# Streamed weights repacked in DRAM, so that rows which the 16 DMA engines are thought to move together lie side by side

## Chip, cores, metric

One core of a Trainium2 chip. The metric is the time of one execution on the device, in microseconds (us). All runs whose times are compared here are in the fast state (the probe e5, a single run, is read from its profile alone), and all outputs agreed with the reference.

## The reference, cut to what matters

Two branches over the same 2048 tokens of width 640, mixed by a gate. Branch A is sliding-window attention. Branch B is the one that matters: 64 segments of 32 tokens, each with 8 memory rows that come from the segment before, so the segments run one after the other, each through all of the weights.

```python
for s in range(n_seg):                                # 64 serial steps
    h = concatenate([mem, xs], axis=1)                # 40 rows x 640
    q = einsum('btd,dhe->bhte', h, Wq)                # 640 x (32*192); Wk, Wv alike
    ...
    o = einsum('bhte,hed->btd', o, Wo)                # (32*192) x 640
    mem = o[:, :M, :]                                 # goes into the next step
return g * a + (1 - g) * b
```

## The kernel before

Wq, Wk, Wv and Wo, in bfloat16, are not all kept in SBUF. Most tiles of 128 rows stay resident; 21 (11 of q, k and v, 10 of o) are packed once into a DRAM tensor, and every step loads them again, from the sync engine's queue into a ring of four slots.

```python
WQ, WO = 4 * 384, 2 * D                # 1536 columns (3072 B a row), 1280 (2560 B a row)

class Weights:
    def __init__(self, nc, dram, Wq, Wk, Wv, Wo, streamed):
        ...
        self.packed = dram.tile([len(streamed), P, WQ], BF, name="w_packed")

    def copy(self, u, dst, engine):
        kind, g, c = u
        if kind != "o":
            engine.dma_start(dst, self.src[kind][c, :, g * WQ:(g + 1) * WQ])
            return
        for r in range(2):
            i, b = divmod(2 * c + r, 3)
            for a in range(2):
                engine.dma_start(dst[64 * a:64 * a + 64, r * D:(r + 1) * D], self.Wo[8 * g + 2 * i + a, 64 * b:64 * b + 64, :])

    def dram_of(self, u):
        return self.packed[self.slot[u], :, 0:self.width(u)]
    ...

# in branch_B
    sb = {
        "w": (4, [P, WQ]), ...                     # the ring: 4 slots
    }
    def load_w(u):
        if u not in weights.slot:
            return None
        b = sc.buf("w")
        sc.op("SP", 100 + 0.78 * weights.width(u), lambda: nc.sync.dma_start(tile_of(b)[:, 0:weights.width(u)], weights.dram_of(u)),
              writes=[b])
        return b

STREAMED = {"q": ((4,), (4,), (4,), (4,)), "k": ((4,), (4,), (4,), (4,)), "v": ((), (4,), (4,), (4,)),
            "o": ((2, 5), (1, 3, 5), (1, 3, 5), (2, 5))}
```

Of the kernel before, what the change touches and what calls it, by code (L numbers as in the profile page):

```python
# [9 lines left out]
BF = mybir.dt.bfloat16  # L10
# [252 lines left out]
P = 128  # L263
KT = 5
D = 640


class Sched:
# [9 lines left out]
    def __init__(self, bufs):  # L278
        self.bufs, self.made, self.ops = bufs, {t: [] for t in bufs}, []
# [85 lines left out]
WQ, WO = 4 * 384, 2 * D  # L365
# [3 lines left out]
class Weights:  # L369
# [5 lines left out]
    def __init__(self, nc, dram, Wq, Wk, Wv, Wo, streamed):  # L375
        self.nc = nc
        self.src = {k: W.rearrange("(kt p) h e -> kt p (h e)", p=P) for k, W in (("q", Wq), ("k", Wk), ("v", Wv))}
        self.Wo = Wo
        self.slot = {u: n for n, u in enumerate(streamed)}
        self.packed = dram.tile([len(streamed), P, WQ], BF, name="w_packed")  # L380
        self.resident = [(k, g, c) for k in KINDS for g in range(4) for c in range(PARTS[k]) if (k, g, c) not in self.slot]
        self.tiles = {}

    def copy(self, u, dst, engine):
        kind, g, c = u
        if kind != "o":
            engine.dma_start(dst, self.src[kind][c, :, g * WQ:(g + 1) * WQ])
            return
        for r in range(2):
            i, b = divmod(2 * c + r, 3)  # L390
            for a in range(2):
                engine.dma_start(dst[64 * a:64 * a + 64, r * D:(r + 1) * D], self.Wo[8 * g + 2 * i + a, 64 * b:64 * b + 64, :])

    def load_resident(self, pool, u, engine):
        t = pool.tile([P, self.width(u)], BF, name="w_%s%d%d" % u)
# [5 lines left out]
        return WO if u[0] == "o" else WQ  # L401

    def dram_of(self, u):
        return self.packed[self.slot[u], :, 0:self.width(u)]

    def pack(self, u, engine):
        self.copy(u, self.dram_of(u), engine)

    def get(self, ring, u):
        if u in self.tiles:  # L410
# [59 lines left out]
def branch_B(ctx, tc, xa_dram, xbqk, xbv, mem0, weights, xo_dram):  # L470
    nc = tc.nc
# [49 lines left out]
    sc = Sched({t: n for t, (n, _) in sb.items()} | {t: n for t, (n, _) in kept.items()} | ps)  # L521

    def tile_of(b, shape=None, dtype=BF, name=None):
        t = b["tag"]
        if b["tile"] is None:
            if t in kept:
                b["tile"] = still[t][b["n"] % kept[t][0]]
            elif t in sb:
                b["tile"] = pools[t].tile(sb[t][1], BF, name=f"t_{t}", tag=t)
            else:  # L530
                b["tile"] = pools[t].tile(shape, dtype, name=name or f"p_{t}", tag=t)
        return b["tile"]
# [28 lines left out]
    def load_w(u):  # L561
        if u not in weights.slot:
            return None
        b = sc.buf("w")
        sc.op("SP", 100 + 0.78 * weights.width(u), lambda: nc.sync.dma_start(tile_of(b)[:, 0:weights.width(u)], weights.dram_of(u)),
              writes=[b])
        return b

# [18 lines left out]
    def chunk(kind, s, g):  # L587
        hT = hts[s][0]
        b = sc.buf("mm")
        wb = [load_w((kind, g, kt)) for kt in range(KT)]  # L590
        kts = [kt for kt in range(KT) if wb[kt] is None] + [kt for kt in range(KT) if wb[kt]]

        def f(kt):
            t = tile_of(b, [P, 512], FP32, f"ps_{kind}")
            w = w_of((kind, g, kt), wb[kt])
            for j in range(4):
                nc.tensor.matmul(t[32 * j:32 * j + 32, 0:384], lhsT=tile_of(hT)[:, kt, :], rhs=w[:, j * 384:(j + 1) * 384],  # L597
                                 start=(kt == kts[0]), stop=(kt == kts[-1]), tile_position=(0, 32 * j))
        for kt in kts:
            sc.op("PE", 160, lambda kt=kt: f(kt), reads=[hT] + [wb[kt]] * (wb[kt] is not None), writes=[b], name=(kind, s, g, kt), mode=32)  # L600
        tok = sc.buf("vtok" if kind == "v" else "tok")
        sc.op("ACT", act(384), lambda: nc.scalar.copy(tile_of(tok)[:], b["tile"][:, 0:384]), reads=[b], writes=[tok])  # L602
        made[kind, s, g] = tok
# [145 lines left out]
    def oproj(s, g):  # L749
        OT = made.pop(("O", s, g))  # L750
        if g == 0:
            obufs[s] = sc.buf("o")
        o_b = obufs[s]
        wb = [load_w(("o", g, c)) for c in range(6)]

        def f(c):
            t = tile_of(o_b, [P, 512], FP32, "ps_o")
            w = w_of(("o", g, c), wb[c])
            for r in range(2):
                i, b = divmod(2 * c + r, 3)  # L760
                for dt in range(KT):
                    nc.tensor.matmul(t[:, dt * L:(dt + 1) * L], lhsT=w[:, r * D + dt * P:r * D + (dt + 1) * P],  # L762
                                     rhs=OT["tile"][:, b, i, :], start=(g == 0 and c == 0 and r == 0 and dt == 0),
                                     stop=(g == 3 and c == 5 and r == 1), skip_group_check=True)
        for c in range(6):
            sc.op("PE", 10 * 25.4, lambda c=c: f(c), reads=[OT] + [wb[c]] * (wb[c] is not None), writes=[o_b], name=("o", s, g, c),
                  mode=128)
        if g < 3:
            return
        ov = lambda: o_b["tile"][:, 0:KT * L].rearrange("p (k l) -> p k l", l=L)  # L770
        if s + 1 < nseg:
            hT, xl = hts[s + 1]
            sc.op("DVE", dve(40), lambda: nc.vector.tensor_copy(tile_of(hT)[:, :, 0:MEM], ov()[:, :, 0:MEM]), reads=[o_b], writes=[hT],  # L773
                  after=[xl])
        oT = sc.buf("oT")
        sc.op("ACT", act(160), lambda: nc.scalar.copy(tile_of(oT)[:], ov()[:, :, MEM:L]), reads=[o_b], writes=[oT])
        sc.op("DMA", 500, lambda: nc.gpsimd.dma_start(xo_dram[s], oT["tile"][:].rearrange("p k t -> p (k t)")), reads=[oT])
# [152 lines left out]
```

## Time and profile before

| | before |
|---|---|
| time, median of 4 runs | 2607.56 us (2599.64 to 2622.13) |
| recurrent stage (700 to 2590 us): TensorE busy, DMA share, GB/s | 1634 us of 1890, 0.86, 274 |
| weight tiles loaded in it | 1344, one every 1.40 us |
| TensorE's waits for them | 152 us |
| row of 3072 B: median, mean | 121 ns, 154.8 ns |

The profiled execution took 2625.68 us, 18 us over the median of the four. "DMA share" is the mean busy share of the core's 16 DMA engines. The row times come from the trace's packet records, which give queue, size, start and duration of each packet, but neither engine nor address. The prediction shows the lines of the profile and reads them.

### The profile page before, as it was taken

The numbers are of one execution on the slowest core, as the hardware profiler recorded it, in microseconds if no ns is written. First come the engines' busy times: TensorE is split into PE (matmuls) and PEld (weight loads), VectorE is DVE, ScalarE is ACT, GpSimd is POOL, SyncE is SP. The second block draws the span as 40 slices with busy tenths as digits, with TensorE's granted clock in tenths as the row PEclk, the third lists the DMA queues.
The fourth block names the chain that finished last, engine by engine and source line by source line (L and its number), as shares of the span: only waits on it lengthen the run. The fifth ranks groups of instructions, "written<-read, shape, count | busy, mean of one in ns | idle before, by whom it ended". The sixth has DMA issues, their size and how long they took to land.

```text
span 2624.0 us, 113795 instructions
## 1 busy us (share of the span) xinstructions
PE 2259.0 (86%) x49877; PEld 1665.6 (63%) x49893; DVE 1189.0 (45%) x3578; ACT 1115.8 (43%) x2433; POOL 602.1 (23%) x1782
## 2 busy tenths in 40 slices
PE   7888888899788888888888888888888888888885
PEld 5777777699465666666655665666666665566663
DVE  5777777623243344434443343434443444334433
ACT  5777777722233333333333333333333333334333
POOL 7622222040122222222222222222222222122220
PEclk9999999999899999989999998999999999999997
DMA  6600000085588888888888888888888888888887
GB/s 215 196 17 17 20 17 15 21 262 150 158 277 264 284 276 264 288 275 281 266 276 271 284 268 266 274 282 275 270 285 272 275 282 273 264 269 283 279 274 236
DMA packets 299154, 591.76 MB, mean 226 GB/s; under 512 B 102552, under 2 KB 112032, under 8 KB 298656
## 3 DMA queue, kind: packets, MB, share of 16 engines
q1 hardware_dynamic: 275536, 525.43, 63.6%
q0 software_dynamic: 20160, 55.60, 6.5%
q8 instruction: 391, 6.41, 1.0%
q10 hardware_dynamic: 2960, 3.44, 0.4%
q14 instruction: 107, 0.88, 0.1%
HBM read 554.98 MB, written 36.97 MB: 226 GB/s over the span
## 4 chain that ended last, share of the span: by engine, by line
PE 51%; DMA 35%; ACT 10%; DVE 2%; issue 2%; SPq 0%; ACTq 0%; POOL 0%; DVEq 0%
DMA t_w<-w_packed 32%; PE ps_q L597 8%; PE ps_k L597 8%; PE ps_o L762 7%; PE ps_v L597 5%; ACT a_ex L195 4%; PE t_psum L438 4%; ACT a_pt L208 3%; PE qk_ps L124 3%; PE ps_pv L738 2%; PE tr_k L612 2%; PE t_psv L455 2%; PE S_ps L666 2%; PE pt_ps L205 1%; PE s_ps L187 1%
## 5 line engine op out<-in xcount | busy, mean ns | idle before, releaser
L597 PEld LDWEIGHTS <-t_hT 128*32 128x32 bf16 x15360 | 380.0, 99 | 310.2 <-issue 105.8
L762 PE MATMUL ps_o<-t_OT,t_w 128*128 128x40 bf16 x6400 | 270.6, 182 | 124.9 <-DMA t_w<-w_packed 113.7
L762 PE MATMUL ps_o<-t_OT,w_o 128*128 128x40 bf16 x8960 | 334.6, 182 | 42.0 <-ACT t_OT L743 41.7
L762 PEld LDWEIGHTS <-w_o 128*128 128x128 bf16 x8960 | 289.1, 98 | 49.5 <-issue 43.5
L762 PEld LDWEIGHTS <-t_w 128*128 128x128 bf16 x6400 | 210.6, 98 | 155.4 <-DMA t_w<-w_packed 152.1
L743 ACT CAST t_OT<-ps_pv 128x480 bf16<-128x480 f32 x256 | 143.2, 559 | 340.2 <-PE ps_pv L738 339.9
L195 ACT ACTIVATE a_ex<-s_ps,a_nmx 128x384 bf16<-128x384 f32 (+2 forms) x512 | 252.8, 576 | 64.2 <-DVE a_nmx L193 61.5
L644 POOL COPY t_K<-t_xqk 128x64 bf16<-128x64 bf16 x256 | 60.8, 237 | 947.8 <-PE S_ps L666 665.6
L193 DVE TENSOR_REDUCE a_nmx<-s_ps 128x1 f32<-128x384 f32 (+2 forms) x512 | 246.7, 523 | 32.4 <-PE s_ps L190 24.8
L602 ACT CAST t_tok<-ps_k 128x384 bf16<-128x384 f32 x256 | 122.7, 479 | 319.5 <-PE ps_k L597 319.5
L597 PE MATMUL ps_q<-w_q,t_hT 128*32 128x384 bf16 x4096 | 230.4, 348 | 18.7 <-DVE t_hT L773 18.4
L721 DVE TENSOR_TENSOR t_PTx<-PT_ps,mk_x 128x320 bf16<-128x320 f32 x256 | 125.2, 489 | 264.7 <-PE PT_ps L714 264.7
L597 PE MATMUL ps_v<-w_v,t_hT 128*32 128x384 bf16 x4352 | 230.1, 335 | 0.0
L597 PE MATMUL ps_k<-w_k,t_hT 128*32 128x384 bf16 x4096 | 226.3, 343 | 0.3
L635 DVE COPY t_K<-tr_k 128x256 bf16<-128x256 bf16 x256 | 74.0, 289 | 253.7 <-PE tr_k L612 252.4
L602 ACT CAST t_tok<-ps_q 128x384 bf16<-128x384 f32 x256 | 123.0, 481 | 137.7 <-PE ps_q L597 137.5
L187 PE MATMUL s_ps<-KT_blk,QTm 128*128 128x128 bf16 x1440 | 171.0, 223 | 6.0 <-ACT a_ex L195 5.6
L602 ACT CAST t_vtok<-ps_v 128x384 bf16<-128x384 f32 x256 | 122.7, 479 | 114.2 <-PE ps_v L597 112.9
L612 PEld LDWEIGHTS <-t_tok 128*128 128x128 bf16 x1536 | 87.7, 98 | 118.7 <-ACT t_tok L602 55.4
L773 DVE CAST t_hT<-ps_o 128x40 bf16<-128x40 f32 x63 | 12.6, 200 | 327.1 <-PE ps_o L762 327.1
L205 PE MATMUL pt_ps<-a_ident,a_ex 128*128 128x128 bf16 x1440 | 145.6, 220 | 8.5 <-ACT a_ex L195 1.2
L676 DVE TENSOR_REDUCE sm_mx<-S_ps 128x4 f32<-128x160 f32 x256 | 82.5, 322 | 149.0 <-PE S_ps L666 149.0
(138 smaller groups left out, 4606.2 us busy)
## 6 DMA issues: line engine op xcount, KB each, us to landing
t_w<-w_packed SPq DMA_DIRECT2D x704, 384.0 KB, 4.4
t_w<-w_packed SPq DMA_DIRECT2D x640, 320.0 KB, 4.3
xbqk<-t_qk SPq DMA_DIRECT2D x16, 768.0 KB, 5.1
t_xqk<-xbqk POOLq DMA_DIRECT2D x64, 192.0 KB, 4.7
w_v<-in_B_Wv_dram POOLq DMA_DIRECT2D x17, 384.0 KB, 7.1
w_q<-in_B_Wq_dram POOLq DMA_DIRECT2D x16, 384.0 KB, 5.2
w_k<-in_B_Wk_dram POOLq DMA_DIRECT2D x16, 384.0 KB, 6.5
xbv<-t_vt SPq DMA_DIRECT2D x64, 96.0 KB, 1.8
```

The source lines that it names most:

```text
L187: nc.tensor.matmul(sp[:, ci * P:(ci + 1) * P], lhsT=qm[r][:, g, :], rhs=kring[c][:, g, :], start=True, stop=not need_mask)
L193: nc.vector.tensor_reduce(out=nmx[:], in_=sp[:, 0:nk * P], axis=AX.X, op=ALU.max, negate=True)
L195: nc.scalar.activation(out=ex[:, 0:nk * P], in_=sp[:, 0:nk * P], func=ACT.Exp, bias=nmx[:], scale=1.0)
L205: nc.tensor.transpose(pt_ps[:, a, ci, :], ex[:, ci * P:(ci + 1) * P], ident[:])
L438: nc.tensor.matmul(pt[:, bb, :], lhsT=ws[ki][kt][:, c:c + P], rhs=xTb[:, kt, t * P:(t + 1) * P], start=(kt == 0), stop=(kt == KT - 1))
L597: nc.tensor.matmul(t[32 * j:32 * j + 32, 0:384], lhsT=tile_of(hT)[:, kt, :], rhs=w[:, j * 384:(j + 1) * 384], start=(kt == kts[0]), stop=( ...
L602: sc.op("ACT", act(384), lambda: nc.scalar.copy(tile_of(tok)[:], b["tile"][:, 0:384]), reads=[b], writes=[tok])
L612: nc.tensor.transpose(t[:, k, :], tok["tile"][:, k * P:(k + 1) * P], ident[:])
L676: nc.vector.tensor_reduce(out=x["mx"][:], in_=view(), axis=AX.X, op=ALU.max)
L721: nc.vector.tensor_tensor(out=tile_of(dst)[:], in0=PT["tile"][:, i, :, :].unsqueeze(2).to_broadcast([P, 2, 4, L]), in1=mk.unsqueeze(1).uns ...
L743: sc.op("ACT", act(480), lambda: nc.scalar.copy(tile_of(OT)[:].rearrange("p b j l -> p (b j l)"), o["tile"][:, 0:480]), reads=[o], writes= ...
L762: nc.tensor.matmul(t[:, dt * L:(dt + 1) * L], lhsT=w[:, r * D + dt * P:r * D + (dt + 1) * P], rhs=OT["tile"][:, b, i, :], start=(g == 0 an ...
```

## The change

The change takes it that a tile's 128 rows are divided over 16 DMA engines, 8 rows each, and that engine e moves rows 8e to 8e+7. It stores row 8e+a at place 16a+e, so that the rows that the 16 engines would then read at the same moment are one piece of 48 KB in DRAM. The load then reads with the pattern (16, 8, columns) and still writes 128 partitions in their order.

```diff
-        self.packed = dram.tile([len(streamed), P, WQ], BF, name="w_packed")
+        self.packed = dram.tile([len(streamed), 8, 16, WQ], BF, name="w_packed")
...
-    def copy(self, u, dst, engine):
+    def copy(self, u, dst, engine, packed=False):
...
-                engine.dma_start(dst[64 * a:64 * a + 64, r * D:(r + 1) * D], self.Wo[8 * g + 2 * i + a, 64 * b:64 * b + 64, :])
+                part = slice(8 * a, 8 * a + 8) if packed else slice(64 * a, 64 * a + 64)
+                engine.dma_start(dst[part, ..., r * D:(r + 1) * D], self.Wo[8 * g + 2 * i + a, 64 * b:64 * b + 64, :])
...
     def dram_of(self, u):
-        return self.packed[self.slot[u], :, 0:self.width(u)]
+        return self.packed[self.slot[u], :, :, 0:self.width(u)].rearrange("a e c -> e a c")

     def pack(self, u, engine):
-        self.copy(u, self.dram_of(u), engine)
+        self.copy(u, self.dram_of(u), engine, True)
```

More of the change, by code (lines that the diff above doesn't have):

```diff
@@ L564, in load_w @@
         b = sc.buf("w")
-        sc.op("SP", 100 + 0.78 * weights.width(u), lambda: nc.sync.dma_start(tile_of(b)[:, 0:weights.width(u)], weights.dram_of(u)),
+        sc.op("SP", 100 + 0.78 * weights.width(u), lambda: nc.sync.dma_start(
+            tile_of(b)[:, 0:weights.width(u)], weights.dram_of(u)),
               writes=[b])
```

## The prediction

"Port conflict" and "the ports" in it, and "port theory" in what was expected of the runs, stand for an assumption: that with the new pattern engines hold each other up in pairs, that a row takes twice as long while a pair is in step, and that this is so half of the time. No trace had shown it. The factors 2 and 1.5 are guesses; what they multiply is from the trace, 18.8 us a step at the steady rate and 4.9 us of stalls, which make the 23.7 us of a step in which no pair is in step.

> **What bounds the kernel now.** I read the slices of the page first, then the chain, then a table by stage, then the waits and the view of the streamed weight tile. The page has three stages: a sliding-window attention (to about 520 us), projections (to 700 us), and 64 serial steps of the recurrent branch, where the DMA engines are busy from end to end:
>
> ```profile
> span 2624.0 us, 113795 instructions
> ...
> PEclk9999999999899999989999998999999999999997
> DMA  6600000085588888888888888888888888888887
> GB/s 215 196 17 17 20 17 15 21 262 150 158 277 264 284 276 264 288 275 281 266 276 271 284 268 266 274 282 275 270 285 272 275 282 273 264 269 283 279 274 236
> ...
> q1 hardware_dynamic: 275536, 525.43, 63.6%
> ...
> PE 51%; DMA 35%; ACT 10%; DVE 2%; issue 2%; SPq 0%; ACTq 0%; POOL 0%; DVEq 0%
> DMA t_w<-w_packed 32%; PE ps_q L597 8%; PE ps_k L597 8%; PE ps_o L762 7%; PE ps_v L597 5%; ACT a_ex L195 4%; PE t_psum L438 4%; ACT a_pt L208 3%; PE qk_ps L124 3%; PE ps_pv L738 2%; PE tr_k L612 2%; PE t_psv L455 2%; PE S_ps L666 2%; PE pt_ps L205 1%; PE s_ps L187 1%
> ```
>
> A third of the chain is one transfer, the load of a streamed weight tile. The table by stage (length; busy time and instructions of PE, PEld, DVE, ACT and POOL; granted clock, DMA share, GB/s) for the recurrent stage:
>
> ```profile
> 700.00:2590.00 1890.00, 1634.09 (x40453) 1140.43 (x40453) 750.80 (x2627) 690.83 (x1603) 399.04 (x1369) 0.94 0.86 274
> ```
>
> So 29.5 us a step, TensorE busy 25.5 of them. What it waits for on the streamed tiles, and the tile's own view:
>
> ```profile
> PE ps_o L762 <- DMA t_w<-w_packed: 113.7, 178, 2.1
> PE ps_q L597 <- DMA t_w<-w_packed: 17.5, 24, 2.0
> PE ps_v L597 <- DMA t_w<-w_packed: 12.5, 23, 1.6
> PE ps_k L597 <- DMA t_w<-w_packed: 8.7, 19, 1.2
> ```
>
> ```profile
> L565 SPq DMA_DIRECT2D t_w<-w_packed x1344: 319/320/1599, 699.0 to 2583.7; - x192
> ...
> DMA to landing us min/median/max: 2.7/4.3/7.5
> ```
>
> The four waits sum to 152 us: all that an infinitely fast stream could win. 1344 tiles in 1885 us is one each 1.40 us, and a tile lands 4.3 us after its issue, so some three of the ring's four slots are always on their way. TensorE and the weight stream bound the stage by turns, with little slack in either.
>
> The trace also holds one record per DMA packet. In this stage a row of 3072 B (q, k, v tiles) takes 121 ns at the median and 154.8 on average, a row of 2560 B (o tiles) 102 and 125.7: four of five rows run at a steady rate of 25 GB/s per engine, and the rest stall, for up to about a microsecond. One step moves 11 tiles of the first kind and 10 of the second, 8 rows each per engine: 88 x 121 + 80 x 102 = 18.8 us at the steady rate, 88 x 154.8 + 80 x 125.7 = 23.7 us with the stalls, 0.80 of a step. That and the small traffic make the 0.86.
>
> [...] full-height loads run at the steady rate (the token loads of 128 rows of 1280 B in the attention stage take 55 ns at the median, 62.6 on average), while the resident o weights are loaded 64 partitions at a time,
>
> ```profile
> w_o<-in_B_Wo_dram POOLq DMA_DIRECT2D x56, 80.0 KB, 5.0
> ```
>
> and there, from 575 to 579 us, where these loads come one at a time, a packet of 5120 B takes 283 ns on average against 194 at its fastest: 1.46 times, although their rows are contiguous in DRAM. [...]
>
> **The change part by part.** The built programs have the same instructions in the same order on TensorE, VectorE and ScalarE. Three things move.
>
> First, the row order in DRAM. Row p = 8e + a now lies at a x 16 + e, and the load's source becomes (16, 8, columns) against 128 partitions. For the intent to hold, engine e must move partitions 8e to 8e+7[...]. Then, at the same row of every engine, 16 rows of 3 KB lie side by side. If all stalls came from where rows lie, 4.9 us of engine time a step would go and up to 152 us could be won. But I see no sign that stalls follow the layout: the resident q weights (98 KB between one engine's rows and the next's if eight go to each) show a mean of 1.20 times the steady rate, and the weights in the packed layout 1.28 and 1.23 under heavier load.
>
> Second, and I think larger, the destination. [...] In step, always: 2 x 18.8 + 4.9 = 42.5 us a step. [...] Stalls of some 30 ns a row on average, in lumps, should scatter the pairs, so I take the middle, 1.5 x 18.8 = 28.2; a partner that is itself stalled (21% of its time) does not compete, so of the 9.4 added some 7.5 remain: 26.3 + 4.9 stalls = 31.2. The other traffic adds (0.86 - 0.82) x 29.5 = 1.2, giving 32.4 us of engine time a step. That is above the step of today, so the stream becomes the sole bound, and TensorE's 27 us fit beneath it. No ring of four keeps the engines wholly busy; I estimate 0.93 (0.86 to 0.88 in stretches today where TensorE waits): 34.9 us a step, 64 x 34.9 = 2230 against 1890, so +340 us.
>
> Third, issue and packing. Copies of the sync queue whose two sides have equal dimensions take 320 ns to issue, those with three dimensions 360 to 370[...]. I allow 0.3 us more per issue; 1344 x 0.62 = 830 us fit in the queue, and behind two queued tiles the latency is mostly hidden: +10 us. The copies that pack the weights (51, on GpSimd, in the attention stage[...]) interleave otherwise with its copies; the first read of a packed tile is at 519 us: 0. Sum: 2608 + 340 + 10, about 2960 us.
>
> **The rivals.** (A) The intent: rows side by side end the stalls[...]. For it: a quarter of the engine time is stalls, and four-fifths of the waits are in one place. Against it: the stalls look the same in other layouts. Half of the stalls gone would win perhaps 70 us: 2530. (B) Neither matters: [...] only the dearer issue is left. [...] 0 to 40 us: 2610 to 2650. (C) The port conflict in full[...]: 42.5 + 1.2 = 43.7, at 0.95 some 46 us a step, 2944 us of stage, 3660 in all. [...]
>
> **Range and chances.** The middle, 2960, is the port conflict at half strength; a quarter of full strength gives about 2700 and three quarters about 3300, so 2660 to 3320 covers most of it and touches (B). Faster by over 2% needs (A) without the ports: 0.08. Within 2%: 0.12. Slower: 0.80, for the w_o loads show the conflict in this very kernel.
>
> **What would show it.** Right: rows of 3072 B well over 121 ns at the median (I expect 160 to 200), the DMA share of the stage at 0.92 or more, GB/s of the stage down from 274 to about 230, landing at 5 us or more, the chain mostly t_w<-w_packed, TensorE's waits on it several hundred us, attention stage unchanged. Wrong: a median still at 121 ns. With fewer stalls and landing under 4 us, it was (A); with landing up by only the issue time, (B). A median at 240 is (C).

## The result, and the profile after

2884.22 us median of 4 runs (2880.51 to 2887.19) against 2607.56 us: a ratio of 1.1053, 95% interval 1.1002 to 1.1104. Slower. Ratios here are the mean time of one kernel's fast runs over that of the other's from the same rounds, so not quite the ratio of the medians quoted.

The page after: span, the slices (granted TensorE clock, DMA share, GB/s), the sync queue's packets, and the chain that ended last:

```profile
span 2878.8 us, 113809 instructions
...
PEclk9999999998998999999898898889999899999886
DMA  6211100755998999999999899999999899999987
GB/s 232 77 50 31 34 26 9 226 151 152 243 246 236 244 243 242 251 241 243 245 245 238 234 245 240 237 244 242 242 241 248 236 237 241 244 249 242 243 239 215
...
q1 hardware_dynamic: 275536, 525.43, 69.7%
...
DMA 49%; PE 39%; ACT 8%; DVE 2%; issue 1%; POOL 0%; SPq 0%; ACTq 0%; DVEq 0%; POOLq 0%
DMA t_w<-w_packed 45%; PE ps_q L600 6%; PE ps_v L600 6%; PE ps_o L765 5%; ACT a_ex L195 4%; PE ps_k L600 3%; PE t_psum L440 3%; ACT a_pt L208 3%; PE ps_pv L741 3%; PE qk_ps L124 2%; PE out_ps L255 1%; PE pt_ps L205 1%; PE s_ps L187 1%; PE t_psv L457 1%; DVE a_nmx L193 1%
```

The queue moved the same 275536 packets and 525 MB in more time; the engines were busier in the recurrent stage (DMA share 0.93 against 0.86), yet moved fewer GB/s (241 against 274); and the load's part of the chain went up from 32% to 45%. The recurrent stage by itself (columns as in the prediction):

```profile
700.00:2845.00 2145.00, 1735.21 (x40453) 1190.08 (x40453) 751.36 (x2626) 692.12 (x1602) 394.66 (x1365) 0.90 0.93 241
```

TensorE's waits for the streamed tiles, and the tile's own view:

```profile
PE ps_o L765 <- DMA t_w<-w_packed: 211.5, 242, 2.8
PE ps_k L600 <- DMA t_w<-w_packed: 51.0, 84, 2.7
...
PE ps_q L600 <- DMA t_w<-w_packed: 29.9, 53, 1.8
...
PE ps_v L600 <- DMA t_w<-w_packed: 20.4, 34, 1.3
```

```profile
L567 SPq DMA_DIRECT2D t_w<-w_packed x1344: 514/514/1383, 696.8 to 2836.3; - x192
...
DMA to landing us min/median/max: 3.4/5.5/7.8
```

From the first to the last issue of a weight load the two profiles differ by 2139.5 - 1884.7 = 254.8 us, and the spans by 2878.8 - 2624.0 = 254.8 us. All of the loss between them is in this stage (by the medians the loss is 277 us; the profiled execution of the kernel before was a slow one). The waits went from 152 to 313 us; the other 100 us are TensorE's busy time in the stage, 1634 to 1735 us, at a granted clock of 0.90 instead of 0.94. I do not count that as a second cause: where the stream sets the pace, a faster TensorE would only have waited longer. That is argued and not shown: in the runs below, busy time and waits rise together (e12: 1581 us at a clock of 0.97, with 74 us of waits; e11: 1754 us at 0.87, with 297), and no run changes the one and holds the other. A row of 3072 B now takes 179 ns at the median and 186.3 on average, one of 2560 B 148 and 155.0.

### The profile page after: what moved, and what is told of

The parts are those of the page before. It is cut to its first block, busy times and chain, and to the rows that moved or that the text cites. A ratio compares the mean times of both kernels' runs of the same rounds, so it can differ in the third digit from the quotient of the medians.

```text
span 2878.8 us, 113809 instructions
## 1 busy us (share of the span) xinstructions
PE 2362.2 (82%) x49893; PEld 1712.2 (59%) x49893; DVE 1189.8 (41%) x3578; ACT 1116.8 (39%) x2433; POOL 599.6 (21%) x1782
## 3 DMA queue, kind: packets, MB, share of 16 engines
q1 hardware_dynamic: 275536, 525.43, 69.7%
q10 hardware_dynamic: 2960, 3.44, 0.4%
## 4 chain that ended last, share of the span: by engine, by line
DMA 49%; PE 39%; ACT 8%; DVE 2%; issue 1%; POOL 0%; SPq 0%; ACTq 0%; DVEq 0%; POOLq 0%
DMA t_w<-w_packed 45%; PE ps_q L600 6%; PE ps_v L600 6%; PE ps_o L765 5%; ACT a_ex L195 4%; PE ps_k L600 3%; PE t_psum L440 3%; ACT a_pt L208 3%; PE ps_pv L741 3%; PE qk_ps L124 2%; PE out_ps L255 1%; PE pt_ps L205 1%; PE s_ps L187 1%; PE t_psv L457 1%; DVE a_nmx L193 1%
## 5 line engine op out<-in xcount | busy, mean ns | idle before, releaser
L600 PEld LDWEIGHTS <-t_hT 128*32 128x32 bf16 x15360 | 402.9, 101 | 425.6 <-issue 234.6
L765 PE MATMUL ps_o<-t_OT,t_w 128*128 128x40 bf16 x6400 | 279.3, 186 | 214.5 <-DMA t_w<-w_packed 211.5
L765 PE MATMUL ps_o<-t_OT,w_o 128*128 128x40 bf16 x8960 | 341.7, 184 | 42.4 <-ACT t_OT L746 41.7
L765 PEld LDWEIGHTS <-t_w 128*128 128x128 bf16 x6400 | 217.8, 100 | 246.6 <-DMA t_w<-w_packed 241.9
L765 PEld LDWEIGHTS <-w_o 128*128 128x128 bf16 x8960 | 296.6, 99 | 50.0 <-issue 43.9
L193 DVE TENSOR_REDUCE a_nmx<-s_ps 128x1 f32<-128x384 f32 (+2 forms) x512 | 246.2, 523 | 31.3 <-PE s_ps L190 23.7
L600 PE MATMUL ps_v<-w_v,t_hT 128*32 128x384 bf16 x4352 | 257.0, 365 | 0.0
L741 PE MATMUL ps_pv<-t_PTx,t_xv 128*64 128x160 bf16 x1536 | 154.4, 260 | 0.0
```

The costliest lines, as they stand in the source:

```text
L193: nc.vector.tensor_reduce(out=nmx[:], in_=sp[:, 0:nk * P], axis=AX.X, op=ALU.max, negate=True)
L600: nc.tensor.matmul(t[32 * j:32 * j + 32, 0:384], lhsT=tile_of(hT)[:, kt, :], rhs=w[:, j * 384:(j + 1) * 384], start=(kt == kts[0]), stop=( ...
L741: nc.tensor.matmul(t[64 * a:64 * a + 64, 160 * b:160 * b + 160], lhsT=v[:, c:c + 64], rhs=p["tile"][:, a, :, :].rearrange("p j l -> p (j l ...
L765: nc.tensor.matmul(t[:, dt * L:(dt + 1) * L], lhsT=w[:, r * D + dt * P:r * D + (dt + 1) * P], rhs=OT["tile"][:, b, i, :], start=(g == 0 an ...
```

## The experiments

Each kernel was timed on one chip beside the kernel before. "Row" below is the time of a 3072 B packet in the recurrent stage unless another size is named.

### e1: the dearer issue alone

The kernel is built with a switch that is called the mark of a prepared copy here. What it changes inside a copy no trace shows; what shows is the time of the issue. `unprepared` takes the mark off for the old loads, and their issue then takes 451 ns instead of 320. That the changed loads are unmarked is inferred from their 514 ns, which are also the issue time of the same pattern in the probe e5, where the mark is off.

```diff
+    def unprepared(f):
+        ...
+        f()
+        ...
...
-        sc.op("SP", ..., lambda: nc.sync.dma_start(tile_of(b)[...], weights.dram_of(u)),
+        sc.op("SP", ..., lambda: unprepared(lambda: nc.sync.dma_start(tile_of(b)[...], weights.dram_of(u))),
```

> The kernel before, its rows in the old order and its loads 128 rows against 128 partitions, but built without the mark of a prepared copy on the 1344 weight loads of the recurrent branch, as in the changed kernel. Port theory: issue takes 0.51 us as in the changed kernel (0.32 before), packets of 3072 B stay at 121 ns at the median, landing rises by about 0.2 us from 4.3 us, time 2610 to 2640 us (at most +1.2%). Rival, that the dearer issue is what cost the time: most of +277 us, so about 2850 us.

2636.19 us, ratio 1.0138 (1.0094 to 1.0182). The tile's view:

```profile
L570 SPq DMA_DIRECT2D t_w<-w_packed x1344: 450/451/1541, 700.0 to 2594.4; - x192
...
DMA to landing us min/median/max: 3.0/4.4/7.1
```

An issue takes 451 ns instead of 320 (not the 514 of the changed kernel), the row stays at 121 ns, and 131 ns an issue cost about 36 us. That is about an eighth of the loss. The changed kernel's issue is 194 ns dearer, not 131; in proportion that would be 53 us, a fifth of the loss (an estimate from these figures, for a kernel that still waits for its ring).

### e2: the same pattern of the load, with the rows in the old order

```diff
-        self.packed = dram.tile([len(streamed), P, WQ], BF, name="w_packed")
+        self.packed = dram.tile([len(streamed), 16, 9 * WQ], BF, name="w_packed")
...
-        return self.packed[self.slot[u], :, 0:self.width(u)]
+        return self.packed[self.slot[u], :, 0:8 * WQ].rearrange("e (a c) -> e a c", c=WQ)[:, :, 0:self.width(u)]
```

The ninth row of each group is a gap: without it the 128 rows would lie at one pitch again, as in the kernel before.

> Loads of (16, 8, columns) as in the changed kernel[...], but each engine's 8 rows lie one after the other in DRAM (27 KB from one engine's first row to the next's), as they would in the old order. Port theory: as slow as the changed kernel, 2840 to 2930 us, 3072 B packets at 170 to 190 ns at the median, DMA share 0.93 of the recurrent stage. Rival, that the new row order in DRAM is what slowed the reads: near the kernel before, 2610 to 2660 us, median 121 ns. If rows side by side did end stalls, this kernel is slower than the changed one and shows more packets over 250 ns than its 4.6% (10.4% before).

2905.3 us, ratio 1.1176 (1.1132 to 1.122), row 180 ns at the median. Its tile's view has the issue and the landing of the changed kernel:

```profile
L566 SPq DMA_DIRECT2D t_w<-w_packed x1344: 514/515/1617, 703.9 to 2870.7; - x192
...
DMA to landing us min/median/max: 3.4/5.5/8.8
```

So the loss needs no row to lie where the change put it. It comes with the pattern of the load. One sign speaks for the row order, though: 6.1% of the rows here take over 250 ns, against 5.5% in the changed kernel (and 8.0% before; the 4.6% and 10.4% in the expectation are not what the packet records give).

### e3: the old order, two copies of 64 partitions

```diff
+    def halves(dst, src):
+        for a in range(2):
+            nc.sync.dma_start(dst[64 * a:64 * a + 64], src[64 * a:64 * a + 64])
...
-        sc.op("SP", ..., lambda: nc.sync.dma_start(tile_of(b)[...], weights.dram_of(u)),
+        sc.op("SP", ..., lambda: halves(tile_of(b)[...], weights.dram_of(u)),
```

> The kernel before with its old row order, each weight tile loaded by two copies of 64 partitions[...]. Port theory: [...] packets of 3072 B rise to 170 ns or more at the median, time 2850 to 3300 us. Rival, that DRAM layout or the three-dimensional pattern is the cause: median 121 ns, and the time rises only by twice the issues (1.0 us of issue a tile, still under the 1.40 us a tile takes now), 2620 to 2720 us.

3008.04 us, ratio 1.1571 (1.1528 to 1.1614), row 196 ns at the median. With the old order and a two-dimensional pattern the rows are at least as slow as in the changed kernel (179 ns), once the copy reaches half of the partitions. A part of the time is due to the second copy, and these copies too seem to be without the mark: their issue takes 444 ns at its fastest, as do the halves of the probe e5, where it is off. That is what e6 is for.

```profile
L563 SPq DMA_DIRECT2D t_w<-w_packed x2688: 444/596/1740, 702.5 to 2965.8; - x192
```

### e4: rows 16 KB apart

```diff
-        self.packed = dram.tile([len(streamed), P, WQ], BF, name="w_packed")
+        self.packed = dram.tile([len(streamed), P, 8192], BF, name="w_packed")
```

> The kernel before with its rows 16 KB apart in DRAM instead of 3 KB[...]. If where rows lie in DRAM matters at all at this load, rows this far apart show more and longer stalls: mean of 3072 B packets above 165 ns (154.8 before) and over 2660 us. If the stalls do not follow the layout: 2590 to 2640 us, mean 150 to 160 ns.

2602.32 us, ratio 1.002 (0.997 to 1.0069). The mean row was 142.3 ns, under the range that I had given: rows five times as far apart stalled no more often (5.2% over 250 ns, against 8.0% in the one profile of the kernel before).

### e5: the streams by themselves

Five stretches of 64 tiles (the last in 128 copies) between the recurrent branch and the last stage, into a ring of 8, with no reader.

```diff
+def probe(tc, weights):
+    ...
+    rows = weights.packed[:].rearrange("s p c -> (s p) c")
+    plain = lambda n: weights.packed[n % 8]
+    side = lambda n: weights.packed[n % 8].rearrange("(a e) c -> e a c", e=16)
+    order = lambda n: rows[P * (n % 8):P * (n % 8) + 144].rearrange("(e a) c -> e a c", a=9)[:, 0:8, :]
+    ...
+                if kind == 4:
+                    for a in range(2):
+                        nc.sync.dma_start(t[64 * a:64 * a + 64, :], plain(n)[64 * a:64 * a + 64, :])
+                else:
+                    nc.sync.dma_start(t[:], (plain, plain, side, order)[kind](n))
```

> The kernel before with five stretches of 64 weight-tile loads each put between the recurrent branch and the last stage, into a ring of 8 buffers, with nothing that reads them (the result is unchanged): plain; plain without the mark of a prepared copy; 16 rows side by side as in the changed kernel; the same split with each engine's rows one after the other; two copies of 64 partitions. Here nothing but the DMA engines sets the pace. Port theory: the first two take about 1.1 us a tile (8 rows of 121 ns and some stalls), the other three 1.45 us or more[...]. Rival, rows side by side help and only issue or TensorE spoils it: side is at or under plain. If DRAM order has a share of its own, side and order differ by over 5%.

This kernel ran once, so only the profile counts. Below is a table by stage, with one line for the middle of each stretch in the order of the text (plain; unprepared, which is plain without the mark; side, the rows as the change lays them; order, the rows as in e2; halves); the last two columns are DMA share and GB/s (the share passes 1 because records overlap a little):

```profile
core 0: us, PE busy (x) PEld busy (x) DVE busy (x) ACT busy (x) POOL busy (x), PEclk, DMA share, GB/s
2595.00:2635.00 40.00, 0.00 (x0) 0.00 (x0) 0.00 (x0) 0.00 (x0) 0.00 (x0) 0.50 1.03 401
2655.00:2695.00 40.00, 0.00 (x0) 0.00 (x0) 0.00 (x0) 0.00 (x0) 0.00 (x0) 0.50 1.03 402
2720.00:2790.00 70.00, 0.00 (x0) 0.00 (x0) 0.00 (x0) 0.00 (x0) 0.00 (x0) 0.50 1.04 263
2815.00:2885.00 70.00, 0.00 (x0) 0.00 (x0) 0.00 (x0) 0.00 (x0) 0.00 (x0) 0.50 1.04 265
2910.00:2990.00 80.00, 0.00 (x0) 0.00 (x0) 0.00 (x0) 0.00 (x0) 0.00 (x0) 0.50 1.04 256
```

The engines are full in all five. They move 402 GB/s in the first two stretches and 256 to 265 in the others. By the times between issues, once the ring is full, it is 0.978, 0.978, 1.493, 1.483 and 1.530 us a tile. This is the disputed cost by itself: the pattern of the change is 1.493 / 0.978 = 1.53 times as dear, its row order is worth nothing beside the other one, the issue costs nothing where eight tiles are queued, and 64-partition copies cost nearly the same as the change (1.530).

Two things in the row records were not as I had pictured them. With nothing else at work the plain rows do not stall: 121 to 133 ns from the 1st to the 99th percentile, none of the tail that the same rows have in the recurrent stage (8% over 250 ns). And the slow rows are all slow, 169 to 224 ns in the side stretch; they are not a mix of rows at 121 and at 242. That holds for the probe: in the changed kernel, where the engines are busy 0.93 of the time, 24% of the 3072 B rows still take 118 to 124 ns (81% before), and in e11, at 0.99, 6% do.

### e6: two copies, split by columns

```diff
+    def halves(dst, src, n):
+        ...
+        for a in range(2):
+            nc.sync.dma_start(dst[:, a * n:(a + 1) * n], src[:, a * n:(a + 1) * n])
+        ...
```

> Control for the halves: the kernel before, each weight tile loaded by two copies again, without the prepared mark, but split by columns, 128 partitions each[...]. Port theory: no conflict, so 2650 to 2760 us, the rest being twice the issues and twice the packets of half the size. Rival, that it was the second copy and its issue that cost the halves their 15.7%: 2950 us or more.

The mark is left off because the issue times of e3's halves are those of copies without it; the issues then agree (600 ns at the median, 596 there):

```profile
L564 SPq DMA_DIRECT2D t_w<-w_packed x2688: 450/600/2181, 697.7 to 2747.1; - x192
```

2790.67 us, ratio 1.068 (1.0631 to 1.0729): above the range expected, and well under the halves. Packets of 1536 B take 65 ns at the median and 78 on average, 23.6 GB/s an engine at the median against 25.4 for the rows of 3072 B in 121 ns, so full-height copies nearly keep their rate. The second copy costs more than I had thought (two issues of 600 ns are 1.2 us a tile). Of the halves' ratio, 1.1571 / 1.068 = 1.083 is left for the 64 partitions; the two ran on different chips, so this is rough.

### e7: the change on the o tiles alone

```diff
     def dram_of(self, u):
+        if u[0] != "o":
+            return self.packed[self.slot[u]].rearrange("a e c -> (a e) c")
         return self.packed[self.slot[u], :, :, 0:self.width(u)].rearrange("a e c -> e a c")
```

> The change on the 640 o tiles alone; the 704 q, k and v tiles keep old order, split and issue. Port theory: the cost follows the share of the stream under the conflict, 42% of its bytes, so 30 to 55% of the changed kernel's +277 us: 2680 to 2760 us; 2560 B packets at 140 ns or more, 3072 B packets at 121 ns at the median or little above (beside o packets of the tile before or after). Rival, that a ring of four absorbs it: under 2640 us.

2794.68 us, ratio 1.0692 (1.0645 to 1.0738): two-thirds of the whole loss from 43% of the bytes (640 tiles of 320 KB against 704 of 384; the 42% in the expectation is a slip). I had expected up to 55%, so the cost is not in proportion to the bytes. It fits that the waits are not either: before the change 113.7 of the 152 us were at the o products, where the stream is asked for tiles fastest, and here that line has 207.5 us. That is an argument from the waits; no run separates it. The 2560 B rows took 126 ns at the median and 152 on average, where I had expected 140 or more at the median; the 3072 B rows stayed at 121.

### e8 and e9: row order again, with the same pattern of the load

The changed kernel and the kernel of e2, in the same rounds on one chip.

> The changed kernel again, on the same chip and in the same rounds as e9, to see whether rows side by side are worth anything[...]. The two were 1.1053 and 1.1176 of the kernel before, on separate occasions. If DRAM order matters: this one is faster than e9 by 0.7 to 1.5%. If it doesn't: within 0.5%.

> The kernel of e2 again (each engine's 8 rows one after the other[...]), beside e8. DRAM order matters: 2895 to 2920 us and 0.7 to 1.5% slower than e8. It doesn't: within 0.5% of e8.

2875.16 us (1.1035) and 2888.45 us (1.1085): the mean of the first is 0.5% under that of the second. The six runs of each span 2868 to 2884 and 2880 to 2896 us, so the 13 us, four times their standard error, are probably real, and side by side fewer rows take over 250 ns (4.7% against 6.2%). The row order seems to do a little of what was intended: about 13 us here, against a loss of 270.

### e10 to e12: a fifth and a sixth slot

Two findings point to the ring: 131 ns of issue cost 36 us, and the plain stream can do a tile in 0.98 us while the kernel takes 1.40. So a slot's round trip is on the path, I reasoned. The room in SBUF comes from streaming one more v tile for each slot added.

```diff
-        "w": (4, [P, WQ]), ...
+        "w": (5, [P, WQ]), ...          # e12: 6
-STREAMED = {... "v": ((), (4,), (4,), (4,)),
+STREAMED = {... "v": ((4,), (4,), (4,), (4,)),          # e12: ((4,), (4,), (3, 4), (4,))
```

> A version that may beat both, from e1 (131 ns of issue cost 36 us, so the wait for a slot's next tile is on the path) and from the stream probe (1.0 us a tile when nothing waits for TensorE, against 1.40 in the kernel): the kernel before with a ring of five slots, the room taken from one more v tile that is now streamed (22 tiles a step instead of 21). If latency through the ring holds the stream back: 2500 to 2590 us. If its engines do: 2610 to 2720 us, as the stream is 4.9% larger.

2544.05 us, ratio 0.9756 (0.9718 to 0.9793), although the stream grew by a tile a step.

> The changed kernel with the same five slots and 22 tiles. Port theory: the engines are at 1.5 us a tile whatever waits for them, so a fifth slot does not win the loss back: 2850 to 2980 us (22 x 1.5 x 64 = 2112 us for the stage and about 750 outside). If the change cost time through latency (issue and landing): under 2800 us.

2911.7 us, ratio 1.1191 (1.1136 to 1.1245). The recurrent stage of e11, whose engines are busy 0.99 of the time:

```profile
710.00:2860.00 2150.00, 1753.68 (x40287) 1196.72 (x40287) 749.37 (x2623) 689.28 (x1598) 395.00 (x1357) 0.87 0.99 251
```

From the first issue to the last, 2158.8 us for 1408 tiles are 1.53 us a tile, against 1.49 in the probe where nothing waited for TensorE. The slot that wins 2.4% in the old kernel wins no time here: a tile comes every 1.53 us instead of 1.59, which only pays for the tile more. This is the clearest sign that the changed kernel is near the bound that the engines' rate sets, and that little of its time is latency.

> One step further than e10: six slots and 23 tiles a step, old row order. Latency still on the path: 2490 to 2530 us. The engines, 0.91 busy in the recurrent stage of e10, now set the pace: 2540 to 2600 us, with a DMA share of 0.94 or more.

2514.59 us, ratio 0.9604 (0.9562 to 0.9646), the fastest of all. Its stage:

```profile
700.00:2470.00 1770.00, 1581.17 (x40485) 1117.48 (x40483) 752.94 (x2630) 692.10 (x1607) 400.60 (x1373) 0.97 0.95 321
```

The old rows, with two more slots, move 321 GB/s; the engines are at 0.95, so I expect little more from further slots; a seventh was not tried.

## Why the prediction was right, point by point

Predicted 2960 us, range 2660 to 3320, slower with 0.80; measured 2884.22.

| term | predicted | measured |
|---|---|---|
| rows of 3072 B, median | 160 to 200 ns | 179 ns |
| factor on a row, pattern of the change | 1.5 | 1.53 (e5) |
| engine time of a step's weight rows | 31.2 us | 88 x 186.3 + 80 x 155.0 = 28.8 us |
| DMA share of the stage | 0.93 | 0.93 |
| GB/s of the stage | about 230 | 241 |
| landing | 5 us or more | 5.5 us |
| other traffic of a step | 1.2 us | 2.3 us (1.8 before) |
| longer stage | +340 us | +255 us in the profiles |
| whole time | +350 us | +277 us by the medians |
| dearer issue | +10 us | +36 us for 131 of the 194 ns (e1) |
| packing | 0 | 0 (first weight load at 696.8 us against 699.0) |

- **The destination.** The step held: e2 and e9 move the rows back and keep the loss, e3 gets slow rows with the old order and half of the partitions, e5 shows the factor with nothing else running. What is shown is that the pattern (16, 8, columns), and copies of 64 partitions, cost 1.53 and 1.56 times the plain load's engine time (1.493 and 1.530 us a tile against 0.978, e5). Why they do is not shown: no record names an engine or a partition, and the port conflict is still an assumption. A three-dimensional pattern that divides the destination in another way was not tried. Without it, the pattern and the 64 partitions could each have a cost of their own that happens to be of the same size.
- **The picture behind the 1.5 was wrong in its detail, and that the size came out was in part luck.** I had it as the middle between pairs in step and pairs out of step, rows of 242 ns and of 121. In the probe, where the engines are never idle (DMA share 1.04), the rows are evenly slow (169 to 224 ns), so the engines do not seem to fall in and out of step as whole rows. Whether pairs of engines share anything at all is open.
- **The evidence for it in this kernel was misread.** The 283 ns on average for the packets of the w_o loads are not in the trace. From 575 to 579 us 55 of them start; they take 196 ns at the median, 194 at the fastest, 247 on average and up to 582, so most are not slowed there. "The w_o loads show the conflict in this very kernel" does not stand; e3 and e5 had to show it.
- **The size was too large by a third** (340 for 255 in the profiles; 350 for 277 by the medians), and the term that failed is the engine time of a step's weights, 31.2 us for 28.8. I had added all of the stalls of before, 4.9 us, to the slower rows. In the changed kernel 5.5% of the 3072 B rows take over 250 ns instead of 8.0%; stalls and slower rows do not add up. Half of that excess was cancelled by the other traffic, 2.3 us for 1.2; its 0.82 should have been the 0.80 worked out above it, which gives 1.8. Two more slips: by its own steps three quarters of the conflict give about 3210 us, not 3300, and the longest rows before took 1.8 us, not about one.
- **The issue was undersized**, by thinking that two queued tiles hide it: alone it costs 36 us in a kernel whose ring is on the path, and that for 131 of the 194 ns. In the changed kernel, where the engines are the bound, its share is not separated.
- **Rival A, the intent, fell.** Rows 16 KB apart change nothing (e4), side by side is 0.7% slower than in order in the probe and 0.5% faster in the kernel (e8, e9). Its premise is weakened too: the rows in their old places hardly stall when the core is otherwise idle (121 to 133 ns from the 1st to the 99th percentile, e5), so where they lie is not enough to make them stall. What does is open.
- **Rival B** is worth 1.4% by e1, about 2% if the rest of the dearer issue is added in proportion (an estimate). **Rival C** would have shown rows of 242 ns (twice 121).

## What to carry to other kernels

A pattern chosen for the sake of DRAM order can cost more than the order is worth: here (16, 8, columns) took 1.53 times the engine time of the plain load, whichever way the rows lay (1.53 side by side, 1.52 in order, e5). The runs do not show why. So look at the duration of a row, before and after, at its median and not at its mean alone. Test a layout idea with a few dozen loads that nothing reads, in an idle stretch: it took five stretches of one kernel here to tell issue, order and pattern apart. And where a stream and an engine wait for each other by turns, ask what one more slot in the ring is worth first; here two slots won 4%, even at the price of streaming more.
